# One MLP for eight rows, on four column groups, in the tail of an attention block

## The chip, the cores and the metric

The kernel runs on one core of a Trainium2 chip. The metric is the time of one execution on the device in microseconds (us), as a median of several runs. One execution of each kernel was also profiled, which gives a trace of every instruction with its start and its duration. The span of a trace is about 1.9 us shorter than the time of the same run (409.6 against 411.49 for the kernel before).

## The reference

The input is 2048 rows of 448 numbers. The first half is an attention block with 16 query heads and one shared head for keys and values; the second half scores all rows, picks the best eight, and adds an MLP to those eight alone. The second half is what matters here:

```
def _B_ref(x, w_r, w_gate, w_up, w_down):          # x: layernorm of h, 2048 x 448
    r = x @ w_r                                    # one score per row
    idx = argsort(-r)[:, :8]                       # the best 8 rows of 2048
    x_sel = x[idx]
    y = (silu(x_sel @ w_gate) * (x_sel @ w_up)) @ w_down      # 448 -> 1792 -> 448
    y = y * sigmoid(r[idx])
    return x + scatter_add(zeros, idx, y)
h = x + attention(layernorm(x));  out = h + _B_ref(layernorm(h), ...)
```

The rows are worked on in 16 tiles of 128. The score of a row exists only when its attention output is finished, so the last tile decides late which of its rows are among the best eight.

## The kernel before

The kernel is a list of operations (`G.op`) that a scheduler puts into one fixed order per engine; `pieces` splits a list of matmuls into several operations, `mm(out, weights, moving, first, last)` is a matmul. While the last tile goes through attention, the eight best rows of the other 15 tiles are found and become candidates. They are fetched by multiplying every tile with a one-hot matrix, and get an MLP of their own. The last tile gets an MLP for all of its 128 rows, and a mask afterwards keeps the rows that are really picked.

```
# candidates of the 15 first tiles: fetched by 60 one-hot matmuls, then 15 for the base rows
pieces([mm(psg[0:CK, ch, :], xn[:, t, ch*CK:(ch+1)*CK], oh[:, t, :], t == 0, t == NT1-1)
        for ch in range(NCH) for t in range(NT1)], ...)              # NCH = 4, NT1 = 15
G.op(DV, tensor_copy(xselT, psg))
pieces([mm(ps[0:8, VB, 0:D], oh[:, t, :], outf[:, t, :], ...) for t in range(NT1)], ...)
# their gate and up: the weights are loaded into the array, the 8 rows stream: 112 matmuls of 8 columns
pieces([mm(pt[:, fc, :], w_[0:CK, ch, fc*128:(fc+1)*128], xselT[0:CK, ch, :], ...)
        for w_, pt in ((wg_sb, pg), (wu_sb, pu)) for fc in range(NFC) for ch in range(NCH)], ...)
...                                                                  # SiLU, product, 14 down matmuls
# last tile: 4 transposes, 112 gate and up matmuls of 128 columns, 14 down matmuls, then the mask
for bk, f0, f1 in where:
    pieces([mm(gb[bk][:, f-f0, :], wg_sb[0:CK, ch, f*128:(f+1)*128], xT[0:CK, ch, :], ...)
            for f in range(f0, f1) for ch in range(NCH)], ...)
...
G.op(DV, scalar_tensor_tensor(olast, ps[:, 0, 0:D], wst[:, 8:9], outf[:, t, :], mult, add))
evs.append(dma(out_v[:, t, :], olast, ...))
evs.append(G.op(PO, indirect_dma_start(out=out[0], out_offset=idxu, in_=rows8, ...)))
```

## Time and profile before

| | before |
|---|---|
| median of the first 3 runs | 415.63 us (411.62 to 415.91) |
| span of the profiled run | 409.6 us |
| last softmax exponential of ScalarE ends | 370.02 us |
| from there to the epilogue of the eight rows (404.32) | 34.30 us |
| from there to the end (the tail) | 39.6 us |
| mean granted TensorE clock of the profiled run | 0.980 |

The lines that carry the reading stand in the prediction. They are read like this: the slices show which engine is busy when; the chain of waits tells which work stands one behind the other; the table of stretches tells which clock TensorE was granted. The clock counts because a matmul at half clock takes nearly twice as long: the last projection takes 1.67 us here.

### The profile page before, as it was taken

How to read it: one execution, taken by the hardware profiler on the slowest of the kernel's cores; microseconds unless marked ns; L12 is line 12 of the kernel's file. 1: busy time of each engine (PE TensorE's matmuls, PEld its weight loads, DVE VectorE, ACT ScalarE, POOL GpSimd, SP SyncE). 2: the span in 40 equal slices, each digit the busy share in tenths (PEclk: the TensorE clock that was granted, in tenths of full speed). 3: DMA queues.
4: the chain of work that ended last, by engine and by line, in shares of the span. 5: the costliest groups of instructions: out<-in, count | busy, mean ns of one | idle time of the engine just before them, and what ended most of it. 6: DMA issues, size and time to landing. Idle time of an engine off the chain costs nothing.

```text
span 409.6 us, 9063 instructions
## 1 busy us (share of the span) xinstructions
PE 332.0 (81%) x3741; PEld 124.4 (30%) x3742; DVE 341.0 (83%) x699; ACT 367.1 (90%) x308; POOL 192.7 (47%) x178
## 2 busy tenths in 40 slices
PE   7899888787887878787878788878788768877894
PEld 3453222222232322232322222222223212224582
DVE  6994888989898989898989899898989898966332
ACT  5899999999999999999999999999999989982320
POOL 6420343646565646465564736364656563570001
PEclk9999999999999999999999999999999999997698
DMA  7991000100000000101010101010000001000000
GB/s 213 217 262 56 5 28 3 36 5 26 15 17 24 15 28 3 38 3 39 3 40 3 38 4 39 2 37 5 26 16 16 26 4 38 2 13 15 0 2 22
DMA packets 15781, 14.17 MB, mean 35 GB/s; under 512 B 6061, under 2 KB 12981, under 8 KB 15733
## 3 DMA queue, kind: packets, MB, share of 16 engines
q1 hardware_dynamic: 15701, 13.51, 12.0%
q8 instruction: 32, 0.52, 0.5%
q14 instruction: 16, 0.13, 0.1%
q0 software_dynamic: 32, 0.01, 0.0%
HBM read 11.42 MB, written 2.09 MB: 33 GB/s over the span
## 4 chain that ended last, share of the span: by engine, by line
DVE 55%; PE 25%; ACT 13%; issue 4%; DMA 1%; SPq 1%; POOL 1%; POOLq 0%
DVE Y L838 26%; PE ps L463 24%; ACT P L813 13%; DVE Y L847 10%; DVE st L716 2%; DVE Q L576 2%; DVE Ot L858 2%; DVE hbuf L700 2%; DVE junk L735 2%; DVE bn L702 2%; DVE bn L589 2%; DMA x_sb<-in_A_x_dram 1%; DVE xnT L633 1%; SPq L489 1%; DVE xn L618 1%
## 5 line engine op out<-in xcount | busy, mean ns | idle before, releaser
L813 ACT ACTIVATE P<-ps 128x1536 bf16<-128x1536 f32 (+1 forms) x281 | 354.6, 1431 | 4.9 <-PE ps L463 4.7
L838 DVE TENSOR_SCALAR Y<-ps 128x512 int16<-128x512 f32 x240 | 164.2, 684 | 32.8 <-PE ps L463 32.7
L849 POOL TENSOR_TENSOR Y<-Y,step 128x1024 int32<-128x1024 int32 x60 | 113.5, 1892 | 153.1 <-DVE Y L847 152.6
L463 PE MATMUL ps<-Q,K 32*128 32x512 bf16 x1024 | 110.4, 382 | 63.5 <-DVE Y L838 45.2
L463 PE MATMUL ps<-Y,Vs 128*32 128x512 bf16 x960 | 88.9, 384 | 1.6
L463 PEld LDWEIGHTS ps<-Q,K 32*128 32x128 bf16 x1024 | 33.2, 91 | 177.4 <-ACT P L813 163.7
L847 DVE TENSOR_SCALAR Y<-Y 128x2048 int16<-128x2048 int16 x120 | 81.3, 688 | 0.6
L463 PE MATMUL ps<-P,Vs 128*32 128x512 bf16 x784 | 72.4, 386 | 0.7 <-ACT P L813 0.7
L463 PE MATMUL ps<-zero 128*32 128x512 bf16 (+2 forms) x138 | 43.8, 389 | 1.2 <-DVE zero L482 1.2
L463 PEld LDWEIGHTS ps<-Y,Vs 128*32 128x32 bf16 x960 | 23.2, 94 | 31.6 <-issue 16.2
L463 PEld LDWEIGHTS ps<-P,Vs 128*32 128x32 bf16 x784 | 18.8, 94 | 29.1 <-issue 26.1
L686 POOL TENSOR_TENSOR On<-Ot,Rb 128x256 bf16<-128x256 f32 x30 | 21.2, 728 | 2.4 <-DMA Rb<-l_scr 2.1
L712 POOL TENSOR_TENSOR st<-st,nhalf 128x1 f32<-128x1 f32 x15 | 17.5, 1166 | 2.9 <-DVE st L704 2.9
L1094 POOL DMA_INDIRECT out_dram<-Y,idxu x1 | 1.1, 1115 | 37.2 <-issue 37.2
L463 PE MATMUL ps<-xnT,wq_pad 112*128 112x128 bf16 x256 | 17.4, 220 | 0.0
L463 PE MATMUL ps<-wo_pad,On 128*128 128x448 bf16 x64 | 15.6, 368 | 0.5 <-ACT P L813 0.5
L463 PEld LDWEIGHTS ps<-zero 128*32 128x32 bf16 (+1 forms) x139 | 12.0, 99 | 12.9 <-issue 6.4
L463 PEld LDWEIGHTS ps<-xnT,wq_pad 112*128 112x128 bf16 x256 | 14.4, 98 | 3.6 <-issue 3.4
L730 POOL TENSOR_SCALAR xn<-hbuf,st 128x448 bf16<-128x448 f32 x15 | 15.2, 1011 | 0.0
L700 DVE TENSOR_TENSOR hbuf<-ps,x_sb 128x448 f32<-128x448 f32 x16 | 10.0, 625 | 4.0 <-PE ps L463 4.0
L727 POOL TENSOR_SCALAR x_sb<-hbuf,st 128x448 bf16<-128x448 f32 x15 | 11.6, 771 | 1.9 <-DVE st L716 0.4
L589 DVE BATCH_NORM_STATS2 bn<-x_sb 128x6 f32<-128x448 bf16 x16 | 9.8, 614 | 1.9 <-DMA x_sb<-in_A_x_dram 1.9
(163 smaller groups left out, 218.7 us busy)
## 6 DMA issues: line engine op xcount, KB each, us to landing
Rb<-l_scr SPq DMA_DIRECT2D x14, 256.0 KB
out_dram<-x_sb SPq DMA_DIRECT2D x15, 112.0 KB, 1.7
wg_sb<-in_B_w_gate_dram SPq DMA_DIRECT2D x1, 1568.0 KB, 14.9
wu_sb<-in_B_w_up_dram SPq DMA_DIRECT2D x1, 1568.0 KB, 21.5
wd_sb<-in_B_w_down_dram SPq DMA_DIRECT2D x1, 1568.0 KB, 25.3
x_sb<-in_A_x_dram SPq DMA_DIRECT2D x3, 448.0 KB, 5.8
wq_sb<-in_A_wq_dram SPq DMA_DIRECT2D x2, 196.0 KB, 3.3
wo_pad<-in_A_wo_dram SPq DMA_DIRECT2D x4, 98.0 KB
```

The costliest lines, as they stand in the source:

```text
L463: return lambda e: e.matmul(o, lhsT=l, rhs=r, start=start, stop=stop)
L576: G.op(DV, lambda e: e.tensor_scalar(Q[:, q, :, :].rearrange("p g n -> p (g n)"), ps[:, bank, :], qone[:, 0:1], None, ALU.add), dvt(512), ...
L589: G.op(DV, lambda e, t=t: e.bn_stats(bn6[:, t, :], x_sb[:, t, :]), dvt(D), reads=[("x", t)], writes=[("bn6", t)])
L686: G.op(PO, lambda e, c=c: e.tensor_tensor(On[:, rb, c], Ot[:, rb, c], Rb[:, rb, c], ALU.mult), 750, reads=[("Ot", rb), ("Rb", rb)], writes ...
L700: G.op(DV, lambda e: e.tensor_tensor(hbuf[:, hr, :], ps[:, bank, 0:D], x_sb[:, t, :], ALU.add), dvt(D), reads=[pk(bank), ("x", t)], writes ...
L712: G.op(PO, lambda e: e.tensor_tensor(st[:, t, 4:5], st[:, t, 7:8], nhalf[:, 0:1], ALU.pow), 600, reads=[("st7", t), "nhalf"], writes=[("st ...
L727: G.op(PO, lambda e: e.tensor_scalar(outf[:, t, :], hbuf[:, hr, :], st[:, t, 5:6], st[:, t, 6:7], ALU.mult, ALU.add), 800, reads=[("h", hr ...
L730: G.op(PO, lambda e: e.tensor_scalar(xn[:, t, :], hbuf[:, hr, :], st[:, t, 4:5], st[:, t, 6:7], ALU.mult, ALU.add), 800, reads=[("h", hr), ...
L813: G.op(AC, lambda e: e.activation(P[:, s0:s0 + w, :], ps[:, b0:b0 + w, :], ACT.Exp, bias=-(ZERO + SHIFT) * OCT, scale=OCT), w * 427 + 50, ...
L838: G.op(DV, lambda e: e.tensor_scalar(Y[:, y, 0, q, :].bitcast(I16), ps[:, vb, :], 0.0, 32639.0 - STEP[3], ALU.max, ALU.min), dvt(512), rea ...
L847: done = [G.op(DV, lambda e, c=c: e.tensor_single_scalar(y[c].bitcast(I16), y[0].bitcast(I16), STEP[c], ALU.add), 600, reads=r, writes=[(" ...
L849: G.op(PO, lambda e: e.tensor_tensor(y[3].bitcast(I32), y[0].bitcast(I32), step3[:, 0:1].broadcast_to([128, 1024]), ALU.add), 2050, reads= ...
```

## The change

The intent: pick the eight rows over all 16 tiles first, and then do one MLP for exactly those eight. The candidates' rows come from a copy of the normalized rows in DRAM by one indirect transfer, which can run while the last tile is still being worked on. The gate and up matmuls turn around: the eight rows are loaded into the array (32 columns of it), the weights stream 448 columns at a time, and four such matmuls can run on four column groups of the array at once. Between them stand matmuls against zeros, put there to keep the clock of TensorE up (`last_acc` names the operations after which they may be placed). The diff, cut to its core:

```
+        if self.last_acc and not self.todo[b] and b == max(self.todo):      # zero matmuls in the tail
+            ...
+            for n in (512, 256, 128):
+                if t + n * 0.422 + self.turn("F", c.mode) <= s + 1.0:
+                    o = self.warm_op(n)
...
+        dma(xs_v[:, t, :]..., xx[:, :, t, :], [("xs", t)], ...)             # DRAM copy, tiles 0 to 14
...
+        pieces([mm(hp, ident, x_sb[:, t, :], True, False)], ...)            # residual by an identity matmul
+        for h in range(2):                                                  # last projection in two halves
+            pieces([mm(hp, On[:, rb, g*128:(g+1)*128], wo_pad[:, g, :], False, g == 3)
+                    for g in (2*h, 2*h+1)], ...)
...
-        pieces([mm(psg[0:CK, ch, :], xn[:, t, ...], oh[:, t, :], ...)       # 60 one-hot matmuls
-                for ch in range(NCH) for t in range(NT1)], ...)
-        pieces([mm(ps[0:8, VB, 0:D], oh[:, t, :], outf[:, t, :], ...) for t in range(NT1)], ...)
-        pieces([mm(pt[:, fc, :], w_[0:CK, ch, fc*128:(fc+1)*128], xselT[0:CK, ch, :], ...) ...])
+        G.op(PO, indirect_dma_start(out=both8, in_=xs, in_offset=idxu, ...))         # the gather
...
-    for bk, f0, f1 in where:                                                # MLP of 128 rows
-        pieces([mm(gb[bk][:, f-f0, :], wg_sb[...], xT[0:CK, ch, :], ...) ...])
+    pieces([mm(px[0:CK, ch, :], xn[:, t, ...], oh[:, 0, :], ch == 0, False) for ch in range(NCH)], ...)
+    pieces([mm(px[0:CK, ch, :], both8[:, ...], oh[0:8, 1, :], False, ch == NCH-1) for ch in range(NCH)], ...)
+    wide = lambda bank, w_, name: [G.op(PE, [
+        mm(ps[32*c:32*c+32, bank, 0:448], xselT[0:CK, ch, :], w_[0:CK, ch, c*448:(c+1)*448],
+           ch == 0, ch == NCH-1) for c in range(4)], ...) for ch in range(NCH)]
+    wide(gbank, wg_sb, "wg_sb")
+    wide(ubank, wu_sb, "wu_sb")
...                                                       # SiLU, product, transposes, 16 down matmuls
+    G.op(DV, scalar_tensor_tensor(rows8, ps[0:8, dbank, 0:D], fin[:, 1:2], base8, mult, add))
```

## The prediction

> **What bounds the kernel now.** I read the activity by slice first, to see where the kernel changes character.
>
> ```profile
> PE   7899888787887878787878788878788768877894
> ...
> DVE  6994888989898989898989899898989898966332
> ACT  5899999999999999999999999999999989982320
> ...
> PEclk9999999999999999999999999999999999997698
> ```
>
> Each digit is a tenth of a 10.24 us slice. ScalarE (ACT) stands at nine tenths until slice 36 and then falls to two or three; its softmax exponentials (L813) are busy 354.6 us and wait only 4.9 us in all. So the first 370 us are bound by ScalarE, and the last exponential ends at 370.02 us (timeline of ScalarE). From there to the end of the span, 409.6 us, lies a tail of 39.6 us in which no engine is saturated: a chain. I then read the chain that ended last from 365 us on, whose columns are start, duration, engine, tile, line and count.
>
> ```profile
> 370.52 0.70 DVE Ot L858
> ...
> 371.27 1.14 PE ps L463 x2
> ...
> 373.68 8.53 PE ps L463 x74
> ...
> 382.23 0.19 DVE xselT L909
> ...
> 382.50 3.50 PE ps L463 x9
> ...
> 389.02 11.85 PE ps L463 x233
> ...
> 401.47 2.83 PE ps L463 x14
> ...
> 404.32 0.68 DVE Y L1088
> ```
>
> TensorE (PE) owns most of it. The tail does two MLPs: one for all 128 rows of the last tile (only 0 to 8 of them are needed, but which ones is not known before), one for 8 candidates of the other 15 tiles. The 8.53 us piece holds the last projection, delayed behind small row matmuls, and 60 one-hot matmuls that fetch candidates. The 11.85 us piece holds gate, up and down for 128 rows and the candidates' gate and up. The last table is the busy time per stretch:
>
> ```profile
> 370.00:375.00 5.00, 3.15 (x18) 1.92 (x18) 2.93 (x12) 1.28 (x4) 0.00 (x0) 0.80 0.04 4
> 375.00:380.00 5.00, 5.00 (x45) 4.17 (x43) 2.64 (x11) 0.41 (x2) 0.00 (x0) 0.50 0.01 3
> 380.00:385.00 5.00, 4.72 (x31) 2.98 (x31) 2.24 (x13) 2.14 (x4) 0.00 (x0) 0.50 0.00 0
> 385.00:390.00 5.00, 4.17 (x39) 2.31 (x38) 1.04 (x2) 0.65 (x1) 0.00 (x0) 0.84 0.00 0
> 390.00:395.00 5.00, 5.00 (x93) 5.00 (x91) 1.38 (x2) 2.07 (x4) 0.00 (x0) 1.00 0.01 3
> ```
>
> Columns: PE, PEld, DVE, ACT, POOL busy, then granted PE clock. In 375 to 385 us the clock is 0.50: the one-hot matmuls and the last projection run at half speed. VectorE (DVE) works in order, so the LayerNorm of the last tile also waits: its scale is ready on ScalarE at 379.24, but the instruction that uses it (L714) stands behind the candidates' copy (L909, 382.23) and starts at 382.60.
>
> **What the Trainium skill says.** (1) "TensorE: Matmul & The Clock Gate", Part 1, What's actually happening: about 3.4 us without activity halve the clock, about 3.4 us of activity restore it. The trace agrees in kind: matmuls thin out from 366 us, 0.50 from 373, 1.00 again from 387. (2) "TensorEngine Tiling (Array Packing)", Tiling Modes, Key Properties: tiles of the array run in parallel. The trace has it: four 128x32 products of 512 columns (P,Vs) take 0.40 us, twelve 0.83, so 0.215 us more per four. (3) "DMA: Bandwidth & Descriptors", Anatomy of one DMA: a fixed cost of some 2.0 us, mostly the write receipt. Here the 0.5 KB row of candidates took 2.0 us to landing, the indirect write 2.7. (4) "ScalarE: Activation LUTs", What ACT_TABLE_LOAD costs: about 1283 ns for the load; the trace shows 1.28 us.
>
> **The change part by part.** Instruction order of both programs agrees up to the last two blocks (same exponentials, same score matmuls), so I leave 370 us unchanged and rebuild the tail from it. Durations are those of the trace before; hand-offs between engines 0.04 to 0.1 us.
>
> *Removed:* 60 fetching matmuls and 15 for the rows (5.72 us and 4.84 us busy at half clock), 4 transposes and their copy, 112 gate/up matmuls of 128 columns (6.6 us), 112 of 8 columns (3.2 us), one of two down passes of 14 (2.81 us each), two of three full-size epilogues.
>
> *Added off the path:* 15 copies to DRAM of 224 KB each (3.4 MB over some 350 us, against a queue moving 35 GB/s), one gather of 8 rows by POOL, two products on VectorE in place of POOL, zero matmuls that hold the clock up.
>
> *The new tail*, in us after 370.0:
> 1. Last values 0.45; accumulator copy in halves, 0.37 each (0.69 was the whole): 0.9 and 1.2. Sum broadcast, FP32: 1.14 for the whole, so about 0.65 for the first half: 1.6, and 2.05 for the second.
> 2. ScalarE does one 0.2 us exponential for the candidates first, then Ln, Exp, Ln, Exp on 256 columns at about 0.4 each (0.17 fixed plus 256 at 1.2 per ns): 3.4. VectorE's first product finishes early, the second stands behind two copies of candidates' results at about 4.2, so ends at 4.55. Here I chose the pessimistic order.
> 3. Two projection matmuls at full clock (four took 0.93 warm, so some 0.55 for two): 5.15. Residual is already in PSUM, so the 0.62 us add is gone. Statistics 0.63 and 0.18: 6.0.
> 4. Ln and Exp on one column (0.2 each, with hand-offs 6.5) beside the 0.68 + 0.08 router dot: 6.75. Five short dependent VectorE steps of about 0.19, of which two overlap: 7.25. Rank matmul 0.25 beside the 8-wide compare; rank compare 0.35 + 0.08: 8.05; one-hot 0.2: 8.25.
> 5. One-hot for fetched rows needs one more compare of 0.42 and 0.2 and small steps: 9.1. Eight small matmuls in two groups, copy 0.19: 9.65.
> 6. Gate: 16 matmuls on four column groups are four waves of 448 columns, 0.19 each plus 0.17 drain: 10.65; up ends at 11.45 while SiLU runs (224 columns, 0.35 each).
> 7. Two products (0.39 each, pitch 0.3), transposes, then the 0.61 copy of base rows stands ahead of the transposes' copies in VectorE's order: 12.7; first copy 0.3: 13.0.
> 8. Down: 16 matmuls of 448 columns at 0.19 plus 0.17: 16.25. Epilogue 0.67: 16.95.
> 9. Indirect write: before, it went from 405.00 (epilogue ended) to 409.6 (span ended), 4.6 us: 21.6.
>
> So the tail is about 21.6 us in place of 39.6, and the span about 391.6, a saving of 18.0. The profiled execution had 409.6 of span for 411.5 of time, 1.9 more: 393.5 for a run like that one.
>
> **The rivals.**
> *The gather is late.* Its index is ready at about 4.65. An indirect transfer began 1.05 after its input was ready and landed 2.7 later: 8.4, against the one-hot's 9.1. Only 0.7 us of slack. It also waits for the DRAM copy of tile 14, which queues on SP behind two candidate transfers of 0.9 us issue each (369.35 and 370.31): copied out from about 370.3, landed near 372.5. If the gather takes 2 us more than the write did, the end moves by 1.3 us: 395.
> *The clock still falls.* Row order shows about 30 zero matmuls in the tail, yet each wait is a guess of the program's schedule. At half clock steps 3, 6 and 8 lose about 5 us: 398.5. For: it fell before. Against: the fillers are placed just there.
> *The body pays.* Last block's Y add on POOL is moved behind tile 14's statistics and could reach the last values' matmuls late; DRAM copies sit ahead of some broadcasts in SP's order. The add takes 1.89 us and I put its end at 367.9, two us early; POOL waited 2.1 us in all for broadcasts. Cost if wrong: 1 to 3 us.
> *TensorE was hidden and VectorE is the bound.* About half of the new tail is short dependent VectorE and ScalarE steps of 0.2 to 0.7; twenty hand-offs, each 0.05 us longer, add 1 us.
>
> **Range and chances.** Most errors lengthen the tail, by 1 to 5 us; less waiting at the end of the body (ScalarE idles 1.1 us in its last three units) or an easier step 2 shortens it by 2. The three runs before lie at 411.62, 415.63 and 415.91, so a run can be 4 us longer, and a median can fall in either. I put 394.5, between 393.5 and the slower kind at 397.5; 389.5 to 400 holds it 8 times in 10. Two per cent is 8.3 us below 415.63; to miss it, more than half of the 18 us must be lost: faster 0.96, within 0.035, slower 0.005.
>
> **What would show it right or wrong.** Right: last exponential near 370, gate and up about 1.8 us together in waves of 0.19 at clock 1.00, one down pass of about 3.2 us, no instruction waiting for the gather, 4.6 us after the epilogue. Wrong: granted clock 0.50 in gate or down; the four fetched-row matmuls waiting for a DMA; ScalarE waiting in the last block; a tail near 27 us or more. The prediction also fails if four column groups do not run together: gate and up would take 32 times 0.19, 6 us.

## The result, and the profile after

| | before | after |
|---|---|---|
| median of 4 runs | 413.62 us (411.31 to 415.91) | 393.08 us (392.32 to 394.32) |
| span of the profiled run | 409.6 us | 392.5 us |
| last exponential ends (E) | 370.02 us | 370.78 us |
| from E to the start of the epilogue | 34.30 us | 16.77 us |
| from E to the end | 39.6 us | 21.7 us |

The ratio is 0.9506, with a 95% interval of 0.9432 to 0.9581. Ratios in this document are the mean time of one kernel's fast runs over that of the other's of the same rounds, so not quite the ratio of the medians that are quoted. The medians lie 20.5 us apart, the two traces only 17.1: the kernel before was traced in one of its shorter runs (411.49 us), and what the longer ones lose on top is seen in no trace.

The slices of the kernel after (9.8 us each) show the tail now in the last two and a half:

```profile
PE   8899887878787888878787878888787878788794
...
ACT  5799999999999999999999999999999999799850
...
PEclk9999999999999999999999999999999999799999
```

ScalarE is still the bound up to 370 us. The clock no longer falls in the tail; it dips once in the body (slice 35, both in PEclk and in ACT), which not every run of this kernel has: the runs with a mean clock of 1.000 took 392.32 and 392.99. Every trace of this document except that of the kernel before has such a dip near 337 us.

The chain of waits of the kernel after, from the last exponential on (start, duration, engine, tile, line, count):

```profile
370.83 0.72 PE ps L478 x5
...
371.57 0.44 DVE Ot L937
...
372.05 4.11 PE ps L478 x25
...
376.18 0.64 DVE bn L783
...
378.70 0.37 DVE junk L1095 x2
...
380.25 2.97 PE ps L478 x45
...
383.83 3.69 PE ps L478 x19
...
387.55 0.68 DVE Y L1148
```

The 8.53 us and 11.85 us pieces of TensorE are gone. What is left is 4.11 us up to the statistics (L783), a stretch of short VectorE steps that rank and pick (376.18 to 380.11), 2.97 us that hold the end of the row fetch, gate and up, and 3.69 us for the down pass with what stands in front of it. The table of stretches, with the columns PE, PEld, DVE, ACT, POOL busy, then the granted clock:

```profile
370.00:375.00 5.00, 4.11 (x30) 2.25 (x30) 2.92 (x16) 2.47 (x6) 1.65 (x3) 1.00 0.24 71
375.00:380.00 5.00, 4.65 (x26) 1.95 (x24) 4.06 (x23) 2.57 (x6) 1.22 (x1) 1.00 0.04 6
380.00:385.00 5.00, 4.86 (x59) 2.65 (x59) 3.52 (x17) 1.27 (x3) 0.00 (x0) 1.00 0.09 26
```

The clock is 1.00 throughout, where it was 0.80, 0.50 and 0.50 before. The timeline of TensorE (start, busy time, line, operation, operands, count) has the three wide groups, and the timeline of POOL the two indirect transfers:

```profile
380.96 0.94 PE L478 MATMUL ps<-wg_sb,wq_sb 112*32 112x448 bf16 x16
381.71 0.94 PE L478 MATMUL ps<-wu_sb,wq_sb 112*32 112x448 bf16 x16
...
384.32 3.19 PE L478 MATMUL ps<-wd_sb,Y 112*8 112x448 bf16 x16
```

```profile
376.47 1.22 POOL L978 DMA_INDIRECT Y<-x_scr,idxu  x1 [4.83 <-issue]
389.22 0.92 POOL L1150 DMA_INDIRECT out_dram<-Y,wq_sb  x1 [11.52 <-DVE Y L1148]
```

Sixteen matmuls of 448 columns take 0.94 us in gate and in up, but 3.19 us in the down pass, where they go into one column group one after the other. The gather starts at 376.47 and lands 2.5 us later, near 378.97; the first matmul that uses it starts at 380.25. It is hidden by 1.3 us.

### The profile page after: what moved, and what is told of

Same layout as the page of the kernel before. It is cut to its first block, busy times and chain, and to the rows that moved or that the text cites. A ratio compares the mean times of both kernels' runs of the same rounds, so it can differ in the third digit from the quotient of the medians.

```text
span 392.5 us, 8604 instructions
## 1 busy us (share of the span) xinstructions
PE 319.9 (82%) x3501; PEld 110.6 (28%) x3501; DVE 338.5 (86%) x695; ACT 366.7 (93%) x307; POOL 193.4 (49%) x180
## 3 DMA queue, kind: packets, MB, share of 16 engines
q1 hardware_dynamic: 19781, 16.95, 15.8%
## 4 chain that ended last, share of the span: by engine, by line
DVE 60%; PE 23%; ACT 12%; issue 4%; POOL 0%; POOLq 0%
DVE Y L910 28%; PE ps L478 22%; ACT P L885 12%; DVE Y L919 11%; DVE st L752 2%; DVE Q L596 2%; DVE hbuf L730 2%; DVE Ot L932 2%; DVE junk L766 2%; DVE bn L734 2%; DVE bn L609 1%; DVE xnT L653 1%; DVE xx L638 1%; DVE mv L735 1%; DVE K L670 1%
## 5 line engine op out<-in xcount | busy, mean ns | idle before, releaser
L919 DVE TENSOR_SCALAR Y<-Y 128x2048 int16<-128x2048 int16 x120 | 82.3, 696 | 0.6
L478 PE MATMUL ps<-zero 128*32 128x512 bf16 (+3 forms) x162 | 51.4, 395 | 1.2 <-DVE zero L497 1.2
L713 POOL TENSOR_TENSOR On<-Ot,Rb 128x256 bf16<-128x256 f32 x28 | 19.8, 727 | 15.2 <-DMA Rb<-l_scr 15.2
L478 PEld LDWEIGHTS ps<-zero 128*32 128x32 bf16 (+1 forms) x162 | 14.4, 101 | 14.8 <-issue 7.5
L758 POOL TENSOR_SCALAR xx<-hbuf,st 128x448 bf16<-128x448 f32 x15 | 15.6, 1041 | 0.0
L755 POOL TENSOR_SCALAR xx<-hbuf,st 128x448 bf16<-128x448 f32 x15 | 11.2, 746 | 1.6
L730 DVE TENSOR_TENSOR hbuf<-ps,xx 128x448 f32<-128x448 f32 x15 | 9.4, 623 | 2.3 <-PE ps L478 2.3
L596 DVE TENSOR_SCALAR Q<-ps,qone 128x512 bf16<-128x512 f32 x15 | 11.2, 744 | 0.0
L752 DVE SCALAR_TENSOR_TENSOR st<-mv,st 128x1 f32<-128x1 f32 x15 | 11.1, 738 | 0.0
## 6 DMA issues: line engine op xcount, KB each, us to landing
wu_sb<-in_B_w_up_dram SPq DMA_DIRECT2D x1, 1568.0 KB, 20.5
```

The source lines that it names most:

```text
L478: return lambda e: e.matmul(o, lhsT=l, rhs=r, start=start, stop=stop)
L596: G.op(DV, lambda e: e.tensor_scalar(Q[:, q, :, :].rearrange("p g n -> p (g n)"), ps[:, bank, :], qone[:, 0:1], None, ALU.add), dvt(512), ...
L713: G.op(PO, lambda e, c=c: e.tensor_tensor(On[:, rb, c], Ot[:, rb, c], Rb[:, rb, c], ALU.mult), 750, reads=[both[h], rk[h]], writes=[("On", ...
L730: G.op(DV, lambda e: e.tensor_tensor(hbuf[:, hr, :], ps[:, bank, 0:D], x_sb[:, t, :], ALU.add), dvt(D), reads=[pk(bank), ("x", t)], writes ...
L752: G.op(DV, lambda e: e.scalar_tensor_tensor(st[:, t, 6:7], mv[:, t, 0:1], -1.0, st[:, t, 4:5], ALU.mult, ALU.mult), 80, reads=[("mv", t), ...
L755: G.op(PO, lambda e: e.tensor_scalar(outf[:, t, :], hbuf[:, hr, :], st[:, t, 5:6], st[:, t, 6:7], ALU.mult, ALU.add), 800, reads=[("h", hr ...
```

## The experiments

Twelve runs were made, on three chips, two of them of the kernel after as it is, each beside runs of the kernel before. Instants are given as us after E, the end of the last exponential in the same trace, because E itself moves between runs: three profiles of the unchanged kernel after have it at 370.78, 370.54 and 369.31, and all 14 traces lie between 369.07 and 370.96. The same kernel's medians in its three sets of runs are 393.08, 393.43 and 392.77.

### The control (ctl_after)

The changed kernel as it is (ctl_after), five rounds, on the same chip as a_nofill, a_serial and a_best. The kernels of the other two chips are compared by their ratios to the kernel before.

> The changed kernel once more, unedited, as the yardstick of this call: 392.3 to 394.3 us, with a profiled tail of about 21.7 us from the last exponential of ScalarE to the end of the span.

It took 393.43 us (392.89 to 394.13), ratio 0.9501 (0.9461 to 0.9541). The epilogue of its trace starts at E + 16.79, that of the first trace at E + 16.77: the tail repeats to a few hundredths.

### Was the saving the clock's? The zero matmuls removed (a_nofill)

```
-    G.last_acc = [] if exact else ot[-2:]
+    G.last_acc = []
```

> The changed kernel without the zero matmuls of its tail. Theory (they keep the clock at 1.00): the granted clock falls to 0.50 near 374 us, as before the change; the projection's last pair, gate, up and down run at half speed for at least a part, 3 to 5 us more. Rival (the tail's own matmuls are enough, or its chain is made of VectorE and ScalarE steps so that the clock hardly matters): within 1 us, even a little less, as zero matmuls stand in the way of real ones.

It took 396.49 us (394.86 to 397.00) against 393.43. Its table of stretches:

```profile
375.00:380.00 5.00, 1.62 (x14) 1.18 (x13) 4.04 (x22) 3.24 (x6) 1.22 (x1) 0.83 0.04 6
380.00:385.00 5.00, 4.75 (x42) 2.01 (x40) 2.78 (x13) 0.61 (x2) 0.00 (x0) 0.50 0.08 26
385.00:390.00 5.00, 4.83 (x16) 1.69 (x16) 0.41 (x3) 0.00 (x0) 0.00 (x0) 0.65 0.03 8
```

TensorE is busy 1.62 of 5 us while the rows are picked, and the clock that gate and up then find is 0.50: gate takes 1.68 us in place of 0.94, up 1.73, down 4.83 in place of 3.19. So the zero matmuls are worth 3 us net, the lower end of the 3 to 5 expected; the clock fell later than expected, after 378 us and not near 374, so the projection still ran at full clock. Their price is visible too: without them the statistics started at E + 5.03, with them at E + 5.40, as some stand in front of work that was ready.

### Do four column groups run at once? Two experiments (a_serial, a_onegroup)

First the same 32 matmuls in another order in the program: the four of one group one after the other, so that neighbours in the order compete for one group.

```
     mm(ps[32*c:32*c+32, bank, 0:448], xselT[0:CK, ch, :], w_[0:CK, ch, c*448:(c+1)*448], ...)
-    for c in range(4)], 189, ...) for ch in range(NCH)]
+    for ch in range(NCH)], 4 * 189, ...) for c in range(4)]
```

> The changed kernel with the same 32 gate and up matmuls in another order: all four of one column group, then the next group, so that neighbours share a group and can't run side by side. Theory (the four groups run at once): gate and up take about 16 times 0.19 each in place of 0.94 and 0.94 with some overlap at the borders, 3.5 to 4.3 us more in all. Rival (the array overlaps or pipelines them anyway): within 0.5 us.

My theory fell. The time is 393.83 us (392.79 to 393.98), ratio 0.9505 as against 0.9501 of the control, and the timeline of TensorE has

```profile
380.37 0.97 PE L478 MATMUL ps<-wg_sb,wq_sb 112*32 112x448 bf16 x16
381.12 0.98 PE L478 MATMUL ps<-wu_sb,wq_sb 112*32 112x448 bf16 x16
```

0.97 us for 16, where 0.94 was. The order in the program does not matter at this size (that the chip was given the matmuls in the program's order is taken for granted; no trace shows the column group of a matmul). That left open whether the groups run together at all or a wide matmul is just short. So all 32 were sent to the same 32 columns (a wrong result, relative error over a million):

```
-    mm(ps[32*c:32*c+32, bank, 0:448], ...
+    mm(ps[0:32, bank, 0:448], ...
```

> The reordered gate and up once more, but all 32 matmuls write the same 32 partitions, so the same column group of the array (wrong numbers on purpose). In the reordered run with four groups the first gate matmul to the first product took 1.88 us. Theory (four groups run at once, whatever the order in the program): on one group 16 matmuls of 448 columns last 16 times 0.19, so gate and up about 6.1 us and the end 4.2 us later, near 397.5 us. Rival (the 0.047 us between starts is what a 32-column matmul costs anywhere, groups don't matter): within 0.5 us.

```profile
379.25 3.19 PE L478 MATMUL ps<-wg_sb,wq_sb 112*32 112x448 bf16 x16
382.28 3.19 PE L478 MATMUL ps<-wu_sb,wq_sb 112*32 112x448 bf16 x16
```

3.19 us each, against 0.97 in a_serial, in a single look of 397.15 us (state unknown), near the 397.5 expected. The matmuls of the two kernels differ in their column group alone, so the groups do work side by side: 16 matmuls in one group take 16 times 0.19 us and a rest of about 0.15, on four groups 4 times 0.19 and about the same rest.

### The old form of gate and up, in the new tail (a_stat)

Gate and up as they were: weights in the array, the eight rows stream, 128 matmuls of 8 columns, no transposes.

```
-    wide(gbank, wg_sb, "wg_sb");  wide(ubank, wu_sb, "wu_sb")
+    for pt, w_, name, bank in ((gT[0], wg_sb, "wg_sb", gbank), (gT[1], wu_sb, "wu_sb", ubank)):
+        pieces([mm(pt[0:CK, f, :], w_[0:CK, ch, f*CK:(f+1)*CK], xselT[0:CK, ch, 0:8], ...)
+                for f in range(16) for ch in range(NCH)], ...)                # CK = 112
```

> The changed kernel with gate and up in the old form for 8 rows: the weights stationary, 64 matmuls of 8 columns each, result already transposed, so no transposes and no copies of them. Before the change 112 such matmuls ran at about 28 ns each. Theory (the four column groups are what is gained): gate and up 3.6 us in place of 1.8, less 1.2 for the transposes and copies that fall away, 0.6 to 0.8 us more. Rival (the wide form gives back in transposes all that it gains): equal or up to 0.5 us faster.

It took 403.75 us (400.43 to 405.05), ratio 0.9732 (0.9685 to 0.9779): some 10 us more than the control, not under 1. The timeline and the stretch behind it:

```profile
380.29 5.19 PE L478 MATMUL ps<-wq_sb,wg_sb 112*112 112x8 bf16 x64
385.34 6.11 PE L478 MATMUL ps<-wq_sb,wu_sb 112*112 112x8 bf16 x64
...
392.36 6.13 PE L478 MATMUL ps<-wd_sb,Y 112*8 112x448 bf16 x16
```

```profile
385.00:390.00 5.00, 5.00 (x56) 5.00 (x56) 0.00 (x0) 0.28 (x1) 0.00 (x0) 0.50 0.02 3
```

Two things came together, and the second is a flaw of the experiment. The clock fell to 0.50 although TensorE was busy 5.00 of 5 us. And the weights were loaded 112 columns at a time, where the kernel before loads 128. The Trainium skill, "TensorE: Matmul & The Clock Gate", section Weight-path perf modes — Fast Weight Load (FWL) and DoubleRow, says that the fast way of loading weights is taken when there are 128 weight columns and the type is not FP32. The traces agree: 56 loads and matmuls of 8 columns take 1.54 us with 128 columns (kernel before, full clock, 0.0275 us each), while 60 of them with 112 columns take 3.22 us at full clock (the fill experiment below, 0.054 each). So of the 11.3 us of this gate and up (128 matmuls), some 3.5 would remain with 128-column loads at full clock (128 times 0.0275), another 3.4 are the slower load (128 times 0.054 is 6.9), and the last 4.4 the clock. These three are estimates from the two rates. The experiment does not say what the old form with 128 columns would cost in the new tail; what it shows is that the turned form, with 32 columns a load and wide matmuls, took 0.94 us each for gate and up in the same place, at a clock of 1.00.

### The gather and the DRAM copies taken out (a_nogather)

No copies to DRAM and no gather; the fetched rows are zeros (a wrong result, relative error 0.098).

```
-        dma(xs_v[:, t, :]..., xx[:, :, t, :], [("xs", t)], ...)
-        G.op(PO, indirect_dma_start(out=both8, in_=xs, in_offset=idxu, ...))
+        G.op(PO, memset(both8, 0.0), ...)
```

> The changed kernel without the 15 copies of rows to DRAM and without the gather, the fetched rows being zeros (wrong rows on purpose). Theory (all of it is hidden: the gather landed 1.3 us before its use, the copies use idle queues): within 0.5 us. Rival (the copies slow the body through SP's order or the memories, or the gather ends a wait): 1 to 2 us less.

Up to the epilogue nothing moved: it starts at E + 16.78, after E + 16.77 with the gather, and E is 370.21. So 3.4 MB of copies and the gather cost the path nothing. The copies are not free for the rest, though. POOL's products of the body wait for broadcasts from the same queue, and the pages have (kernel before, after, and this one):

```profile
L686 POOL TENSOR_TENSOR On<-Ot,Rb 128x256 bf16<-128x256 f32 x30 | 21.2, 728 | 2.4 <-DMA Rb<-l_scr 2.1
L713 POOL TENSOR_TENSOR On<-Ot,Rb 128x256 bf16<-128x256 f32 x28 | 19.8, 727 | 15.2 <-DMA Rb<-l_scr 15.2
L713 POOL TENSOR_TENSOR On<-Ot,Rb 128x256 bf16<-128x256 f32 x28 | 19.8, 727 | 0.8 <-DMA Rb<-l_scr 0.6
```

These waits rose from 2.1 to 15.2 us with the change and are 0.6 us without the copies; the rival's mechanism is there, but POOL has the time. Yet the time was 396.39 us (394.67 to 396.53), ratio 0.9568 as against 0.9501, some 3 us more. They lie in one place of its chain of waits, ahead of the last indirect write:

```profile
...
387.73 3.59 issue
...
```

POOL's sequencer takes 3.59 us before it sends the write, as against 0.66 us in the kernel after and 0.71 us in the kernel before. Transfers of the queues that the trace calls instruction lie in that gap, but the kernel after has as many in its last 8.5 us (8 packets, 9 here), so they don't tell the two apart. What makes the gap, I could not settle: the kernel before also has only one indirect transfer and does not pay. For the question of the experiment the chain up to the epilogue is enough, but the sum "without the gather" can't be read from the time.

### The residual added by VectorE again (a_hbuf)

```
-        pieces([mm(hp, ident, x_sb[:, t, :], True, False)], ...)
+        G.op(DV, tensor_tensor(hbuf, pp, x_sb[:, t, :], add), ...)      # after the projection
```

> The changed kernel with the residual of the last tile added by VectorE into SBUF, as before the change, in place of the identity matmul into PSUM. Theory (a 0.62 us step is on the chain, while the identity matmul stands 0.3 us in front of the last values): 0.3 to 0.4 us more in all. Rival (reads of PSUM slow the four later steps that now read SBUF): equal or faster.

It took 394.15 us (393.52 to 394.57). The aggregated statistics were ready at E + 6.65 in place of E + 6.29 (chain of waits, start of the next step), so 0.36 us later, as expected; the add itself takes 0.64 us, but the first copy of the accumulator starts earlier (E + 0.50 against E + 0.79), because the identity matmul no longer stands in front of the last value matmuls. The epilogue starts at E + 17.14, 0.35 us later than in the controls; the ratio of the times, 0.9524 (0.9507 to 0.9541), is too close to 0.9501 to show that.

### Four forced orders, and then fewer zero matmuls (a_best, a_best2)

Four places were mended where an instruction stood behind one that was not urgent: the last products ahead of two copies of candidates' results, the copy of base rows behind the transposes' copies, the identity matmul behind the sum broadcast, and the sigmoid's small steps behind the second one-hot.

```
+                if b == NB - 1 and not exact:
+                    for x in behind:                 # the copies cols and bc
+                        x.deps[o.idx] = False        # now after the product
```

> The changed kernel with four orders forced in its tail: both products of the last block ahead of the copies of the candidates' results on VectorE, the copy of the base rows behind the transposes' copies, the residual matmul behind the sum broadcast, and the sigmoid's small steps behind the second one-hot. Theory (each of these sits on the chain): 0.6 + 0.5 + 0.3 + 0.2, so 1.6 us less, a tail of about 20.1 us. Rival (the waits only move to the gather, which landed at 378.97 in the profile against a use at 380.25, or to the copies' results): less than 0.5 us less. Result must stay correct.

It took 392.94 us (392.23 to 393.61) against 393.43, some 0.5 us less, where 1.6 was expected. The ratios, 0.9488 and 0.9501, don't tell the two apart, but the trace agrees: the epilogue starts at E + 16.25 in place of E + 16.79. The accumulator copy started at E + 0.50 and the second product ended at E + 3.73 in place of 4.60, but the statistics started at E + 5.14 in place of 5.40: zero matmuls still stood in front of both pairs of the projection. So these were removed at three places:

```
-            if self.recent(s) >= self.FLOOR0:
+            if c.name == "nofill" or self.recent(s) >= self.FLOOR0:
```

> The kernel of a_best (four forced orders) without the matmuls against zeros in front of the candidates' row matmuls and of the two pairs of the last projection. Theory: they stood in the way of work that was ready, so the first statistics start 0.3 to 0.5 us earlier after the last exponential (4.7 in place of 5.14) at a clock still 1.00; time 392.3 to 392.8, 0.6 to 1.1 under the changed kernel. Rival: the clock falls in the second half of the tail and the time is 394 or more.

> The changed kernel as it is, on the same chip, to compare a_best2 with: 393.0 to 393.8 at a ratio to the kernel before of 0.950 to 0.956.

The path became shorter as meant: the four projection matmuls now run together, and the statistics start at E + 4.56.

```profile
373.74 0.93 PE L478 MATMUL ps<-wo_pad,On 128*128 128x448 bf16 x4
374.51 2.32 PE L478 MATMUL ps<-zero 128*128 128x512 bf16 x10
```

The epilogue starts at E + 15.66, 1.1 us earlier than in the kernel after (E + 16.79 in its trace). The time does not show it: 392.75 us (391.64 to 393.09) against 392.77 (392.09 to 393.77) of the kernel after (ctl_after2, 0.2 us under the range I gave for it), ratios 0.9493 and 0.9501. The profiled run of this kernel had its last exponential 0.8 us later than the control's (370.15 against 369.31), and its end lay 5.1 us after the start of the epilogue rather than 4.9. Whether six runs each hide a gain of under 1 us, or part of it is given back in the last write, stays open. I don't call it a better kernel.

### How much of the old tail was its clock? The kernel before with zero matmuls (b_fill)

The kernel before, with zero matmuls in the waits of TensorE from the accumulator copy to the first gate matmul, nothing else.

```
+        if self.last_acc and not self.todo[b] and b == max(self.todo):
+            ...                                      # as in the change, until the first gate matmul
+    G.last_acc = [] if exact else ot[-1:]
```

> The kernel before, with matmuls against zeros put into the waits of TensorE in its tail, up to the first gate matmul; nothing else is changed. Theory (the clock alone is worth a part of the saving): the last projection (1.67 us at half clock), the 60 one-hot matmuls (5.72 us) and the 15 row matmuls run nearer to full clock, which takes 4 to 6 us off the chain, to about 408, and the runs lie closer together, because the fall of the clock is what spreads them. Rival (narrow matmuls let the clock fall whatever stands in front of them, as the 128 matmuls of 8 columns did in a_stat): the clock is again near 0.50 in 375 to 385 us and the time is within 2 us of the kernel before.

It took 408.94 us (408.33 to 410.54) against 412.50 of the kernel before in the same rounds, ratio 0.9902 (0.9839 to 0.9965). A line of the kernel before, then its timeline and its stretches:

```profile
376.47 5.72 PE L463 MATMUL ps<-oh,xn 128*112 128x8 bf16 x60
```

```profile
376.42 3.22 PE L480 MATMUL ps<-oh,xn 128*112 128x8 bf16 x60
...
396.99 4.29 PE L480 MATMUL ps<-wd_sb,Y 128*8 128x448 bf16 x14 [0.61 <-DVE Y L938]
```

```profile
375.00:380.00 5.00, 4.95 (x75) 4.11 (x76) 2.93 (x15) 0.41 (x2) 0.00 (x0) 1.00 0.02 3
380.00:385.00 5.00, 4.93 (x38) 2.30 (x39) 3.00 (x13) 2.79 (x4) 0.00 (x0) 1.00 0.00 0
```

The clock stays at 1.00 up to the MLP, the 60 one-hot matmuls take 3.22 us in place of 5.72, and the first full group of gate matmuls starts at E + 14.10 in place of E + 19.00: 4.9 us won. The last down pass then gives 1.5 back: it takes 4.29 us where the kernel before needs 2.81, at a clock of 0.82 in its stretch, although the instructions in front of it are the same as before. Why the clock fell there and not in the kernel before is open. The clock records of the traces hold a candidate that was not tested: in all 14 of them the changes of the clock lie whole multiples of 3.41 us apart, at points that fall on other work from run to run. Here the last 3.41 us before the fall (394.75 to 398.16) hold 1.5 us of matmuls of 8 columns, 0.6 us of idle time and only 1.2 us of the down pass; in the kernel before the stretch with that idle time (400.27 to 403.69) holds 0.5 us of the narrow matmuls and 2.2 us of the down pass, and the clock stayed at 1.00. Net, the epilogue came 3.4 us earlier, and the time 3.6. The rival (narrow matmuls pull the clock down whatever stands in front) fell for this stretch; the theory's 4 to 6 us was right up to the MLP and too high over the whole.

### How much was the MLP of 128 rows? The kernel before without it (b_nomlp)

```
-    pieces([tr(psb[0:CK, 3, ...], xn[:, t, ...]) for ch in range(NCH)], ...)
-    for bk, f0, f1 in where: ...                     # gate, up, down of the last tile
-    evs.append(dma(out_v[:, t, :], olast, ...))
+    evs.append(dma(out_v[:, t, :], outf[:, t, :], ...))
```

> The kernel before without the MLP of the last tile's 128 rows (112 gate and up matmuls of 128 columns, 14 down matmuls, their SiLU and products); the rows of the last tile are then left without their MLP part, wrong on purpose. The candidates' narrow gate, up and down stay. Theory (work and clock hang together): without the wide matmuls of the last tile nothing brings the clock back, the candidates' 112 matmuls of 8 columns take about 10 us at 0.50 and their down pass 5 to 6 us, so that only 4 to 7 us are saved: 406 to 409. Rival (the removed work is worth its own duration at full clock, 6.6 + 2.8 us and the waits around it, and the clock recovers as before): 10 to 15 us saved, 399 to 403.

It took 405.18 us (404.63 to 406.63), ratio 0.9804 (0.9742 to 0.9867): 7.3 us less. The result was correct, presumably because with these inputs no picked row lies in the last tile; the kernel as such is still wrong. Its timeline:

```profile
389.57 1.54 PE L463 MATMUL ps<-xselT,wg_sb 112*128 112x8 bf16 x56 [0.75 <-issue]
...
393.42 5.08 PE L463 MATMUL ps<-wd_sb,Y 128*8 128x448 bf16 x14 [0.70 <-DVE Y L921]
```

The piece of 11.85 us in the chain shrank to 3.15, so 8.7 us of work went; but without the wide matmuls the clock was 0.62 in 390 to 395 us, and the candidates' down pass took 5.08 us in place of 2.81. What is left of the 8.7, 6.4 us, is close to what the epilogue moved (34.30 to 27.58 us after E). The expected size was nearly met (4 to 7; the rival, 10 to 15 with the clock recovering, fell), the way to it only in the down pass (5 to 6 expected): I had expected 10 us for the candidates' gate and up at half clock, and they took 3.2, as in the kernel before.

## Why the prediction was right or wrong, point by point

The prediction was right: 394.5 us against 393.08, inside its range, and by the mechanism it gives; one of its terms, the spread between runs, was not, and two of its small errors cancelled by luck. Its steps, in us after E, against the trace of the kernel after:

| step of the prediction | predicted | measured |
|---|---|---|
| 1 accumulator copy starts | 0.45 | 0.79 |
| 2 second product ends | 4.55 | 4.60 |
| 3 statistics aggregated | 6.0 | 6.25 |
| 4 one-hot of the last tile | 8.25 | 8.60 |
| 5 selected rows copied | 9.65 | 10.03 |
| 6 up ends | 11.45 | 11.87 |
| 7 down starts | 13.0 | 13.54 |
| 8 epilogue ends | 16.95 | 17.44 |
| 9 end | 21.6 | 21.7 |

- **What bounds it, and what was left alone.** "I leave 370 us unchanged" held: E was 370.78, 370.54 and 369.31 in three traces of the kernel after, 370.02 before.
- **The sum of 21.6 us** held to 0.1, by two errors that cancel, which is luck. Step 1 was 0.34 too early: I had not put the identity matmul (0.36 us) in front of the last value matmuls; a_best and a_hbuf, where it doesn't stand there, had the copy at E + 0.50. That error didn't travel, since step 2 had been taken pessimistically. The one that did is in step 3: the statistics start at 5.40, where I had 5.15, because zero matmuls stood in front of and between the halves of the projection (a_nofill has 5.03). Small amounts add up to 0.5 by step 8. Step 9 gave it back: 4.6 us were taken from the kernel before, 4.3 were measured.
- **Four groups at once.** Waves of 0.19, 0.94 us for 16, as written; a_onegroup shows what one group would have cost, 3.19 each.
- **Rival "the gather is late"** fell: 1.3 us of slack, where 0.7 was worked out, and taking it out moved the epilogue by 0.01 us.
- **Rival "the clock still falls"** fell because of the zero matmuls, and was well chosen: without them it comes true. I had put its cost at 5 us, with step 3 in it; 3 were measured, because the clock is still 1.00 at the projection and falls only after 378 us. Gate, up and down take 3.2 us longer together.
- **Rival "the body pays"** was real in kind and cost the path nothing. My claim that the last add on POOL ends at 367.9 was wrong, it ended at 370.24 in the trace; four matmuls waited 0.23 us for it and were done by 370.70, still ahead of E, 370.78. The copies did delay the broadcasts (POOL waited 15.2 us for them in place of 2.1), which POOL could afford.
- **Rival "VectorE is the bound"** was real in kind, and already in the sum: from the start of the statistics to the second one-hot I had 3.95 us (5.15 to 9.1), and 3.93 were measured (376.18 to 380.11). The feared extra 1 us did not come.
- **The reading of the clock** was too kind to the rule it cites. In the trace before, TensorE is never idle for more than 1.0 us between 366 and 373 (and busy throughout until 367, not thinning from 366), yet the clock falls; and from 374 to 386 it is shown as nearly always busy and stays at 0.50, for 13.65 us in all. That zero matmuls hold the clock came out right all the same. Of the 15 row matmuls that I put at half clock, the last six (1.32 us) ran at full clock, which was back at 386.6; that changes nothing.
- **The spread** is the step that failed. I took the 4 us between the runs before for something that a changed kernel may have too ("the slower kind at 397.5"). In 11 runs of the kernel before on one chip, times of 411.04 to 415.97 go with mean granted clocks of 0.980 down to 0.966, while the changed kernel lies within 392.1 and 394.3 in all 16 runs here, at clocks of 0.991 to 1.000 where they were recorded. The spread goes with the fall of the clock, and the change took that away. In b_fill, where zero matmuls hold the clock until the last down pass, four runs lie within 2.2 us. No slow kind of run of the kernel before was traced, so where in it the clock is lost longer is not shown. An estimate from the mean clocks (twice the missing share of the span) gives a slow run about 28 us at half clock and the traced one 16; b_fill and b_nomlp, which share the body of the kernel before, have 3.41 us of it near 337 us, where the trace before has none. The upper end of the range was too wide for that reason, and the point sat 1.4 us high, of which the weight given to the slower kind is 1.0 (394.5 in place of 393.5).

Where the 17.5 us between the two epilogues came from is shown in part: holding the clock in the old tail is worth 4.9 us up to the MLP, and the MLP of 128 rows 8.7 us of chain. Each alone loses some of it again in a down pass at a low clock (3.4 and 6.7 us remain). The two were not run together; if they add, they make 13.6 us, or 10.1 by what remains of each. The other 3.9 to 7.4 us must come from the rest of the change (the fetch of the rows by one gather, the one down pass, the turned gate and up, the last projection in halves), and which of these gives how much is not shown.

## What to carry to other kernels

When a tail has no saturated engine, list its chain and its granted clock together: removing work on TensorE also removes what keeps its clock up, and here either gain alone was partly lost again in the next dense pass. For a handful of rows and wide weights, try the rows in the array and the weights streaming over several column groups: gate and up took 1.7 us together here, where the old form would need 3.5 at full clock by the estimate above, but no transposes after it (not run in the new tail); the order in which the groups were fed needed no tuning. Matmuls against zeros paid in the idle waits (3 us net); where some stood in front of work that was ready, it started later (0.37 us at the statistics).

## What the Trainium skill lacked or had wrong

- "TensorE: Matmul & The Clock Gate", Part 3, The mechanism: it calls matmuls strictly in order in start and end. If a matmul whose column group is busy held up those behind it, and the chip was given the program's order (no trace shows that), the order with four of one group in a row would need about 2.5 us for 16 (an estimate from 0.19 us a matmul); it took 0.97, against 0.94 in the other order.
- The same page, Part 1, What's actually happening: it ties the clock to how busy TensorE has been. It lacks that a TensorE shown as busy for 5.00 of 5 us with matmuls of 8 columns on 112-column weights was granted 0.50, whereas matmuls against zeros do count (393.43 us with them, 396.49 without).
- "DMA: Bandwidth & Descriptors", Anatomy of one DMA: about 2.0 us of fixed cost. An indirect write issued by POOL took 4.3 us from its input to the end of the span (about 1.0 ahead of the transfer, 2.7 to 2.8 to landing in the control runs, the rest after it). That section does not account for the 3.59 us of issue alone in a_nogather.
- "ScalarE: Activation LUTs", What ACT_TABLE_LOAD costs: the load of 1283 ns agrees (1.28 us); of the drain of about 1380 ns beside it nothing is seen here, as the next activation started 0.01 us after the load.
